# Two-block score stages, plain loads of x, paired tangents and a separate last unit in a gated attention and feed-forward kernel

## The chip, the cores and the metric

The kernel runs on one core of one Trainium2 chip. The metric is the time of one execution on the device in microseconds; before the change the median of three runs is 1058.25 us (1052.69, 1058.25 and 1058.3).

The core has a matrix engine (PE), whose weight loads are listed apart (PEld), a vector engine (DVE), a scalar engine for exponentials and tangents (ACT), GpSimd (POOL) and a sync engine (SP). Each runs its own instructions in order. Matrix products land in PSUM, which has eight banks of 128 x 512 f32 values; everything else lives in SBUF. Transfers are issued from the queues of SP and ACT.

## What is computed

Two branches read the same x (2048 rows of 512, bf16) and are mixed row by row with a gate:

```python
x = A_x
g = _sigmoid((x * gate_w).sum(-1, keepdims=True))
a = _A_ref(x, A_wqkv, A_wo)                  # attention: 32 heads of 16
b = _B_ref(x, B_w1, B_w2, B_w3, B_w4)
return g * a + (1 - g) * b
...
# _B_ref
h = _gelu(_layernorm(x, axis=-1) @ w1)
...
# four quarters of h shifted by 1, -1, 2, -2 rows
hs = jnp.concatenate([g0, g1, g2, g3], axis=-1) @ w2
x1 = x + hs
h2 = _gelu(_layernorm(x1, axis=-1) @ w3) @ w4   # inner width 1792
return x1 + h2
```

Branch A is plain softmax attention over all 2048 rows, followed by the product with `wo`.

## The kernel before

Attention is cut into 32 units: 4 chunks of 512 query rows times 8 groups of 4 heads. A unit runs over 16 tiles of 128 key rows, and for each of them over its 4 heads, so it has 64 blocks. A block is one score product of 128 keys by 512 queries, filling one PSUM bank. All 2048 blocks are laid in one row and cut into slots of three (`SB = 3`): 683 slots. A slot's scores (`scores`, L446) fill a stage of three banks; one ACT instruction (L510) takes the exponential of all three into a bf16 tile `pt`. Two stages exist, so scores of slot i+2 can be made once the exponential of slot i is done. `attend` (L466) multiplies four finished blocks with the values into the accumulator `acc`; a column of ones beside the values yields the softmax denominators.

PSUM is thereby full: two stages of three banks, one bank for `acc` (`psA`), one bank (`psG`, tag `gen`) for all other products: the projections of queries, keys and values, the transposes and products of branch B, and the final product with `wo`.

The order on each engine is the order in which the program's text issues instructions. One loop runs over the slots. In each it issues the exponential, the scores of slot i+2, the attends whose blocks are ready, the postponed work that has come due (`run_due`, list `later`), and then `beside`: it takes steps from generators of other work until a credit is used up. The credit is 1.0 a slot for the first 22 slots and 0.47 after. A generator yields the price of the step that it has just issued: 0.45 for two matmuls of 512 columns (`MM2`), so 0.9 for a projection of four; 1.2 in place of the last 0.45 where a tanh follows. `need` runs whatever is missing at once. `early` issues the value and key projections of the first head group, then the other keys, then branch B (`mlp`). Query projections (`urgent`) come at set slots, and a chunk's final products (`out_tile`) when all its units and its part of branch B are there.

Lines that matter here:

- L91 to L95: weights are loaded from ACT's queue; x arrives transposed (`xT`, four chunks) by transposing transfers on SP's queue. L108: x is also loaded plainly, tile by tile (`x_sb`).
- L129 is the product in `proj` (keys, queries and both first products of branch B), L160 the value product; L137, L150 and L165 empty the bank into `kT`, `qT` (two masked copies) and `vp`.
- L175 to L183 (`ln_stats`): mean and variance of 16 row tiles, one after another, then the root. L195 normalizes, L203 transposes on PE, L204 copies out.
- L212 to L225 (`gelu_evac`): gelu of one 128 x 512 block by a tanh on ACT (L221), with four DVE instructions before it and one after.
- L476 to L492 (`finish_unit`): the accumulator is copied to `accsb`; three transfers bring the denominators into a tile 16 wide, their reciprocals out to memory, and these back, spread over 128 partitions as `bcs`; then the unit's result is scaled into `oT`.
- L324 to L333 (`out_tile`): eight products with `wo` for a row tile, the gate mix on DVE (L329, L331), the store.

After the last slot the kernel finishes the last unit and computes the four `out_tile`s of the last chunk.

Of the kernel before, what the change touches and what calls it, by code (L numbers as in the profile page):

```python
# [15 lines left out]
EPS = 1e-5  # L16
# [5 lines left out]
def kernel(  # L22
# [33 lines left out]
    psS = ctx.enter_context(tc.tile_pool(name="psS", bufs=2, space=bass.MemoryType.PSUM))  # L56
    psA = ctx.enter_context(tc.tile_pool(name="psA", bufs=1, space=bass.MemoryType.PSUM))
    psG = ctx.enter_context(tc.tile_pool(name="psG", bufs=1, space=bass.MemoryType.PSUM))
    dpool = ctx.enter_context(tc.tile_pool(name="dram", bufs=1, space=bass.MemoryType.DRAM))
# [4 lines left out]
    opool = ctx.enter_context(tc.tile_pool(name="opool", bufs=25))  # L64
# [3 lines left out]
    gelp = ctx.enter_context(tc.tile_pool(name="gel", bufs=4))  # L68
    stat = ctx.enter_context(tc.tile_pool(name="stat", bufs=2))
    fin = ctx.enter_context(tc.tile_pool(name="fin", bufs=2))  # L70

# [12 lines left out]
    mask = const.tile([P, 2], F32, name="mask")  # L84
    rec_d = dpool.tile([NC_ * NU, 4, CH], F32, name="rec_d")
# [5 lines left out]
    nc.scalar.dma_start(out=wkv[:, :, 0:D], in_=wview(A_wqkv[:, D:2 * D]))  # L91
    nc.scalar.dma_start(out=wq[:], in_=wview(A_wqkv[:, 0:D]))
    nc.scalar.dma_start(out=wkv[:, :, D:2 * D], in_=wview(A_wqkv[:, 2 * D:3 * D]))
    for c in range(NC_):
        nc.sync.dma_start(out=xT[c][:], in_=x_flat[c * CH:(c + 1) * CH, :], transpose=True)  # L95

    make_identity(nc, ident[:])
# [9 lines left out]
    for t in range(NT):  # L107
        nc.sync.dma_start(out=x_sb[t][:], in_=x_flat[t * P:(t + 1) * P, :])  # L108
# [14 lines left out]
    state = {"slot": 0}  # L123
    later = []
    made = set()

# [7 lines left out]
    def k_proj(G, c):  # L134
        ps = psG.tile([P, CH], F32, tag="gen", name="ps_k")
        yield from proj(ps, wkv, slice(G * P, (G + 1) * P), xT[c])
        nc.vector.tensor_copy(out=kT[G][:, c, :], in_=ps[:])  # L137
        made.add(("k", G, c))
        yield MM2
        yield FREE  # L140
# [3 lines left out]
    def q_proj(c, G):  # L144
        ps = psG.tile([P, CH], F32, tag="gen", name="ps_q")
# [10 lines left out]
    def v_proj(t):  # L156
        ps = psG.tile([P, CH], F32, tag="gen", name="ps_v")
# [13 lines left out]
    def ln_stats(tag, res):  # L171
        mv = const.tile([P, NT, 2], F32, name=f"mv{tag}")
        for t in range(NT):
            st = stat.tile([P, 6], F32, tag="bnst", name="st")
            nc.vector.bn_stats(out=st[:], in_=x_sb[t][:])  # L175
            nc.vector.bn_aggr(out=mv[:, t, :], in_=st[:])
            yield 0.4
            yield FREE
        rstd = const.tile([P, NT], F32, name=f"rstd{tag}")
        mhalf = const.tile([P, NT], F32, name=f"mhalf{tag}")  # L180
        nc.gpsimd.memset(mhalf[:], -0.5)
        nc.vector.tensor_scalar(out=rstd[:], in0=mv[:, :, 1], scalar1=EPS, scalar2=None, op0=ALU.add)
        nc.gpsimd.tensor_tensor(out=rstd[:], in0=rstd[:], in1=mhalf[:], op=ALU.pow)  # L183
        for _ in range(4):
            yield 0.6
            yield FREE
        res += [mv, rstd]

    def norm_T(mv, rstd, c, res):
        xnT = xtpool.tile([P, KT, CH], BF16, tag="xnT", name="xnT")  # L190
        xns = []
        for j in range(4):
            t = 4 * c + j
            xn = xnpool.tile([P, D], BF16, tag="xn", name="xn")
            nc.vector.tensor_scalar(out=xn[:], in0=x_sb[t][:], scalar1=mv[:, t, 0:1],  # L195
                                    scalar2=rstd[:, t:t + 1], op0=ALU.subtract, op1=ALU.mult)
            xns.append(xn)
            yield 0.2
            yield FREE
        for kt in range(KT):  # L200
            pt = psG.tile([P, CH], BF16, tag="gen", name="ps_t")
            for j in range(4):
                nc.tensor.transpose(pt[:, j * P:(j + 1) * P], xns[j][:, kt * P:(kt + 1) * P], ident[:])  # L203
            nc.vector.tensor_copy(out=xnT[:, kt, :], in_=pt[:])  # L204
            yield 0.5
            yield FREE
        res.append(xnT)

    def gelu_evac(ps, dst):
        slot = state["slot"]  # L210
        yh = gelp.tile([P, CH], BF16, tag="yh", name="yh")
        nc.vector.tensor_scalar(out=yh[:], in0=ps[:], scalar1=0.5, scalar2=None, op0=ALU.mult)  # L212
        sq = gelp.tile([P, CH], BF16, tag="sq", name="sq")
        nc.vector.tensor_tensor(out=sq[:], in0=yh[:], in1=yh[:], op=ALU.mult)  # L214
        nc.vector.tensor_scalar(out=sq[:], in0=sq[:], scalar1=8.0 * C2, scalar2=2.0 * C1,
                                op0=ALU.mult, op1=ALU.add)
        nc.vector.tensor_tensor(out=sq[:], in0=sq[:], in1=yh[:], op=ALU.mult)  # L217
        th = gelp.tile([P, CH], BF16, tag="th", name="th")

        def tanh():  # L220
            nc.scalar.activation(out=th[:], in_=sq[:], func=ACT.Tanh)  # L221
            later.append((state["slot"] + 2, gate_up))

        def gate_up():
            nc.vector.scalar_tensor_tensor(out=dst, in0=th[:], scalar=1.0, in1=yh[:],  # L225
                                           op0=ALU.add, op1=ALU.mult)

        later.append((slot + 4, tanh))
# [5 lines left out]
    def gate():  # L234
        for t in range(NT):
            scr = gelp.tile([P, CH], BF16, tag="yh", name="scr")
            nc.vector.tensor_tensor_reduce(
                out=scr[:], in0=x_sb[t][:], in1=gw_b[:], scale=1.0, scalar=0.0,
                op0=ALU.mult, op1=ALU.add, accum_out=g_raw[:, t:t + 1])
            yield 0.4  # L240
            yield FREE
        for _ in range(3):
            yield 0.6
            yield FREE
        nc.scalar.activation(out=g_t[:], in_=g_raw[:], func=ACT.Tanh, scale=0.5)
        for _ in range(3):
            yield 0.6
            yield FREE
        nc.vector.tensor_scalar(out=g_fin[:], in0=g_t[:], scalar1=0.5, scalar2=0.5,
                                op0=ALU.mult, op1=ALU.add)  # L250

    def mlp():
# [3 lines left out]
        yield from gate()  # L256
        res = []
        yield from ln_stats(1, res)
        mv1, rstd1 = res
# [3 lines left out]
        for c in range(NC_):  # L263
            res = []
            yield from norm_T(mv1, rstd1, c, res)
            for m in range(KT):
                ps = psG.tile([P, CH], F32, tag="gen", name="ps_1")
                yield from proj(ps, w12, slice(m * P, (m + 1) * P), res[0])
                gelu_evac(ps, hT[:, m, 2 + c * CH:2 + (c + 1) * CH])
                yield 1.2  # L270
                yield FREE
        for _ in range(5):
            yield 0.6
            yield FREE
        shift = [1, -1, 2, -2]
        for t in range(NT):
            ps = psG.tile([P, CH], F32, tag="gen", name="ps_2")
            for j in range(KT):
                c0 = 2 + t * P - shift[j]
                nc.tensor.matmul(ps[:], lhsT=hT[:, j, c0:c0 + P], rhs=w12[:, j, D:2 * D],  # L280
                                 start=(j == 0), stop=(j == KT - 1))
                if j == 1:
                    yield MM2
            nc.vector.tensor_tensor(out=x_sb[t][:], in0=x_sb[t][:], in1=ps[:], op=ALU.add)
            yield MM2
            yield FREE
        res = []
        yield from ln_stats(2, res)
        mv2, rstd2 = res
        for c in range(NC_):  # L290
            res = []
            yield from norm_T(mv2, rstd2, c, res)
            g2T = hgpool.tile([P, FT, CH], BF16, tag="hg", name="g2T")
            for m in range(FT):
                ps = psG.tile([P, CH], F32, tag="gen", name="ps_3")
                yield from proj(ps, w3, slice(m * P, (m + 1) * P), res[0])
                gelu_evac(ps, g2T[:, m, :])
                yield 1.2
                yield FREE
            for _ in range(5):  # L300
                yield 0.6
                yield FREE
            for j in range(4):
                t = 4 * c + j
                ps = psG.tile([P, CH], F32, tag="gen", name="ps_4")
                for m in range(FT):
                    nc.tensor.matmul(ps[:], lhsT=g2T[:, m, j * P:(j + 1) * P], rhs=w4[:, m, :],  # L307
                                     start=(m == 0), stop=(m == FT - 1))
                    if m % 2 and m < FT - 1:
                        yield MM2  # L310
                nc.vector.tensor_tensor(out=x_sb[t][:], in0=x_sb[t][:], in1=ps[:], op=ALU.add)  # L311
                yield MM2
                yield FREE
# [3 lines left out]
    oTs = {}  # L317
    state["mixable"] = 0

    def out_tile(c, j):  # L320
        t = 4 * c + j
        aps = psG.tile([P, CH], F32, tag="gen", name="ps_o")
# [238 lines left out]
```

## Time and profile before

| | us |
|---|---|
| median of three runs | 1058.25 |
| profiled execution, its own time | 1064.77 |
| its span, first to last instruction | 1063.0 |
| first exponential starts | 17.40 |
| last exponential ends | 1037.84 |
| exponentials, 683 | 939.4 busy, 1.568 each on average |
| tanh, 72 of 128 x 512 | 51.9 busy, 0.721 each on average |

A row of the timeline gives start, duration, engine, line, operation, tiles (out<-in) and shapes, then in brackets the idle time ahead of it and who ended it. Neighbours of one kind are merged (x4), and one instruction can begin while the one ahead of it is still in its last part, so a start-to-start distance says more than a duration. In the row of 40 slices each digit is the busy share of one slice (26.6 us) in tenths.

### The profile page before, as it was taken

Reading aid. Unit: us, or ns where it says so; the run is one execution under the profiler, and the core shown is the slowest. Engines: PE = TensorE matmul, PEld = TensorE weight load, DVE = VectorE, ACT = ScalarE, POOL = GpSimd, SP = SyncE. Lnnn points to the kernel's source line nnn. Section 1 sums busy time; section 2 is a strip of 40 time slices with the busy share of each in tenths; the row PEclk is TensorE's granted clock in tenths of the full one; section 3 lists DMA queues with packets and bytes.
Section 4 is the critical chain, followed back from the end, with each engine's and each line's share of the span. In section 5 each row is a group of like instructions: output and inputs, shape, how many; then the busy total and the mean of one; then the engine's idle time right before and its main releaser. Section 6 shows DMA issues by size and latency. Waiting matters only on the chain.

```text
span 1063.0 us, 12795 instructions
## 1 busy us (share of the span) xinstructions
PE 833.5 (78%) x5120; PEld 227.4 (21%) x5120; DVE 371.7 (35%) x749; ACT 963.2 (91%) x757; POOL 13.3 (1%) x30
## 2 busy tenths in 40 slices
PE   4878778877888788779877788877788887787774
PEld 1122212222222121112222112221122222122111
DVE  1123443444423534531244421345421345411002
ACT  2356999999999999999999999999999999999990
POOL 2000001000000100000000000000000000000000
PEclk9997656677679666879998779988779978879556
DMA  9500100000000000000000000000000000000000
GB/s 230 150 0 11 51 11 1 11 11 11 11 9 5 11 11 11 11 11 11 25 8 11 11 11 11 27 16 1 10 11 11 31 11 11 1 11 12 11 10 31
DMA packets 31803, 22.97 MB, mean 22 GB/s; under 512 B 18048, under 2 KB 27136, under 8 KB 31744
## 3 DMA queue, kind: packets, MB, share of 16 engines
q1 hardware_dynamic: 30160, 20.58, 6.7%
q10 hardware_dynamic: 1584, 1.57, 0.6%
q8 instruction: 40, 0.66, 0.3%
q14 instruction: 19, 0.16, 0.1%
HBM read 17.43 MB, written 2.36 MB: 19 GB/s over the span
## 4 chain that ended last, share of the span: by engine, by line
ACT 48%; issue 25%; PE 21%; DVE 4%; DMA 2%; ACTq 0%; DVEq 0%; SPq 0%
ACT pt L510 44%; PE stage L446 6%; PE acc L466 4%; ACT th L221 4%; PE ps_v L160 2%; PE ps L129 2%; PE ps_k L129 2%; PE ps_q L129 2%; PE ps L307 1%; PE ps_t L203 1%; PE ps_o L324 1%; DMA xT<-in_A_x_dram 1%; DVE vp L165 1%; DVE qT L150 1%; DVE kT L137 1%
## 5 line engine op out<-in xcount | busy, mean ns | idle before, releaser
L510 ACT ACTIVATE pt<-stage 128x1536 bf16<-128x1536 f32 (+1 forms) x683 | 939.4, 1568 | 72.3 <-PE stage L446 70.7
L446 PE MATMUL stage<-qT,kT 32*128 32x512 bf16 x2048 | 326.7, 467 | 173.5 <-ACT pt L510 160.3
L466 PE MATMUL acc<-pt,vp 128*17 128x512 bf16 (+1 forms) x2048 | 244.1, 470 | 0.9 <-ACT pt L510 0.5
L446 PEld LDWEIGHTS <-kT 32*128 32x128 bf16 x2048 | 104.3, 94 | 471.8 <-issue 460.0
L129 PE MATMUL ps<-xnT,w 128*128 128x512 bf16 x288 | 111.0, 476 | 3.7 <-DVE qT L150 3.7
L212 DVE TENSOR_SCALAR yh<-ps 128x512 bf16<-128x512 f32 x72 | 49.8, 692 | 154.2 <-PE ps L129 154.2
L466 PEld LDWEIGHTS <-vp 128*17 128x17 bf16 (+1 forms) x2048 | 50.0, 89 | 157.4 <-issue 157.3
L307 PE MATMUL ps<-w,g2T 128*128 128x512 bf16 x224 | 71.9, 409 | 1.5 <-DVE qT L150 1.1
L476 DVE COPY accsb<-acc 128x512 f32<-128x512 f32 x32 | 22.1, 689 | 94.5 <-PE acc L466 94.5
L221 ACT ACTIVATE th<-sq 128x512 bf16<-128x512 bf16 x72 | 51.9, 721 | 0.0
L324 PE MATMUL ps_o<-wo_pad,oT 128*128 128x512 bf16 x128 | 40.6, 419 | 12.6 <-DVE oT L492 6.9
L311 DVE TENSOR_TENSOR x_sb<-x_sb,ps 128x512 bf16<-128x512 bf16 x16 | 11.0, 688 | 104.4 <-PE ps L307 104.4
L492 DVE TENSOR_TENSOR oT<-accsb,bcs 128x512 bf16<-128x512 f32 x32 | 22.0, 688 | 62.8 <-DMA bcs<-rec_d 62.8
L129 PE MATMUL ps_k<-xT,wkv 128*128 128x512 bf16 x64 | 24.8, 497 | 17.5 <-DMA xT<-in_A_x_dram 11.4
L225 DVE SCALAR_TENSOR_TENSOR g2T<-th,yh 128x512 bf16<-128x512 bf16 x56 | 37.9, 676 | 0.4 <-ACT th L221 0.4
L150 DVE TENSOR_SCALAR qT<-ps_q,mask 128x512 bf16<-128x512 f32 x32 | 22.6, 747 | 38.2 <-PE ps_q L129 38.2
L160 PE MATMUL ps_v<-wkv,xT 128*128 128x512 bf16 x64 | 26.5, 529 | 8.8 <-DVE vp L165 7.8
L217 DVE TENSOR_TENSOR sq<-sq,yh 128x512 bf16<-128x512 bf16 x72 | 30.6, 425 | 2.5
L214 DVE TENSOR_TENSOR sq<-yh 128x512 bf16<-128x512 bf16 x72 | 30.6, 425 | 2.5
L204 DVE COPY xnT<-ps_t 128x512 bf16<-128x512 bf16 x32 | 13.6, 425 | 45.9 <-PE ps_t L203 45.8
L129 PEld LDWEIGHTS <-w 128*128 128x128 bf16 x288 | 17.8, 102 | 49.3 <-issue 49.3
L129 PE MATMUL ps_q<-xT,wq 128*128 128x512 bf16 x64 | 25.5, 496 | 1.9 <-DVE kT L137 1.0
(41 smaller groups left out, 255.7 us busy)
## 6 DMA issues: line engine op xcount, KB each, us to landing
bcs<-rec_d SPq DMA_DIRECT2D x32, 256.0 KB
w<-in_B_w_dram SPq DMA_DIRECT2D x2, 1792.0 KB
x_sb<-in_A_x_dram SPq DMA_DIRECT2D x16, 128.0 KB
out_dram<-ot SPq DMA_DIRECT2D x16, 128.0 KB
wkv<-in_A_wqkv_dram ACTq DMA_DIRECT2D x2, 512.0 KB
w<-in_B_w_dram SPq DMA_DIRECT2D x2, 512.0 KB
wq<-in_A_wqkv_dram ACTq DMA_DIRECT2D x1, 512.0 KB
wo_pad<-in_A_wo_dram SPq DMA_DIRECT2D x8, 64.0 KB
```

Of the source, the lines that this page charges most:

```text
L129: nc.tensor.matmul(ps[:], lhsT=wt[:, kt, wsl], rhs=rhs[:, kt, :], start=(kt == 0), stop=(kt == KT - 1))
L150: nc.vector.tensor_scalar(out=qT[:, a, :], in0=ps[:], scalar1=mask[:, a:a + 1], scalar2=None, op0=ALU.mult)
L160: nc.tensor.matmul(ps[:], lhsT=xT[c][:, kt, o:o + P], rhs=wkv[:, kt, D:2 * D], start=(kt == 0), stop=(kt == KT - 1))
L212: nc.vector.tensor_scalar(out=yh[:], in0=ps[:], scalar1=0.5, scalar2=None, op0=ALU.mult)
L214: nc.vector.tensor_tensor(out=sq[:], in0=yh[:], in1=yh[:], op=ALU.mult)
L221: nc.scalar.activation(out=th[:], in_=sq[:], func=ACT.Tanh)
L225: nc.vector.scalar_tensor_tensor(out=dst, in0=th[:], scalar=1.0, in1=yh[:], op0=ALU.add, op1=ALU.mult)
L307: nc.tensor.matmul(ps[:], lhsT=g2T[:, m, j * P:(j + 1) * P], rhs=w4[:, m, :], start=(m == 0), stop=(m == FT - 1))
L324: nc.tensor.matmul(aps[:], lhsT=oTs[(c, u)][:, j * P:(j + 1) * P], rhs=wo_pad[:, u, :], start=(u == 0), stop=(u == NU - 1))
L446: nc.tensor.matmul(st[:, k * CH:(k + 1) * CH], lhsT=kT[G][32 * j:32 * j + 32, cc, o:o + P], rhs=qTs[(c, G)][32 * j:32 * j + 32, a, :], sta ...
L466: nc.tensor.matmul(acc[32 * j:32 * j + M, :], lhsT=lhsT, rhs=pts[i][:, k * CH:(k + 1) * CH], start=(kt == 0), stop=(kt == NT - 1), skip_gr ...
L510: nc.scalar.activation(out=pt[:, 0:w], in_=stages.pop(i)[:, 0:w], func=ACT.Exp, scale=DH ** -0.5)
```

## The change

Eight banks are divided anew at first, and several other parts are rearranged:

- For the first 34 slots (`EARLY`) a slot has two blocks, so the two stages need four banks. The two banks set free (`psX`) serve, with `psG`, the projections: `gen` gives out the three in turn. At slot 34 the pools are closed and the old stages of three banks are opened. There are 694 slots in all.
- Four row tiles of x are loaded first, two on each queue, then the 128 columns of the query and key weights that the first head group needs. The first chunk of `xT` is made by 16 transposes on PE, copied out by ACT and DVE in turn; the other three chunks come by transposing transfers as before. The rest of the weights follows in two more transfers. Fourteen matmuls on a tile of zeros (`idle`) run ahead of the transposes.
- Branch B's gelu works on two blocks at once (`gelu_pair`): DVE and ACT instructions of 1024 columns, issued one, two, five and seven slots later; the tanh writes over its input.
- Statistics, gate sums and normalizations are put on a list (`asides`) of which one entry is issued per slot from slot 34 on; the root is taken per four row tiles. `wait_for` yields empty steps until something is made.
- The credit per slot is 0.6 for the first 34 slots, then 0.36, and 1.0 once branch B is done. A tanh is no longer priced.
- The last chunk's final products sum seven units beside the last unit's slots (into `parts`, f32); the last unit (`finish_all`) has its denominators spread by one f32 matmul with a matrix of ones and zeros (`spread`), reciprocals and products by halves on DVE, and one product per row tile (`last_tile`), each in a PSUM buffer of its own, stored from two queues.

```diff
-    for c in range(NC_):
+    for t in range(4):
+        (nc.sync, nc.scalar)[t % 2].dma_start(out=x_sb[t][:], in_=x_flat[t * P:(t + 1) * P, :])
+    nc.sync.dma_start(out=wq[:, :, 0:P], in_=wview(A_wqkv[:, 0:P]))
+    nc.scalar.dma_start(out=wkv[:, :, 0:P], in_=wview(A_wqkv[:, D:D + P]))
     nc.scalar.dma_start(out=wkv[:, :, D:2 * D], in_=wview(A_wqkv[:, 2 * D:3 * D]))
+    for c in range(1, NC_):
         nc.sync.dma_start(out=xT[c][:], in_=x_flat[c * CH:(c + 1) * CH, :], transpose=True)
+    nc.scalar.dma_start(out=wkv[:, :, P:D], in_=wview(A_wqkv[:, D + P:2 * D]))
+    nc.scalar.dma_start(out=wq[:, :, P:D], in_=wview(A_wqkv[:, P:D]))
...
+    EARLY = 34
+    def gen(name, dtype=F32):
+        state["gen"] += 1
+        if state["young"] and state["gen"] % 3:
+            return psX.tile([P, CH], dtype, tag="x", name=name)
+        return psG.tile([P, CH], dtype, tag="gen", name=name)
...
+    def gelu_pair(w, m, rhs, dst, key):
+        yh = gelp.tile([P, 2, CH], BF16, tag="yh", name="yh")
+        sq = gelp.tile([P, 2, CH], BF16, tag="sq", name="sq")
+        for r in range(2):
+            ps = gen("ps_y")
+            yield from proj(ps, w, slice((m + r) * P, (m + r + 1) * P), rhs)
+            nc.vector.tensor_scalar(out=yh[:, r, :], in0=ps[:], scalar1=0.5, scalar2=None, op0=ALU.mult)
+            if r == 0:
+                yield MM2
+                yield FREE
...
+        def tanh():
+            nc.scalar.activation(out=sq[:], in_=sq[:], func=ACT.Tanh)
+        def gate_up():
+            nc.vector.scalar_tensor_tensor(out=dst, in0=sq[:], scalar=1.0, in1=yh[:], op0=ALU.add, op1=ALU.mult)
+            made.add(key)
+        slot = state["slot"]
+        later.extend([(slot + 1, square), (slot + 2, inner), (slot + 5, tanh), (slot + 7, gate_up)])
+        yield MM2
+        yield FREE
...
+    def last_tile(j, aps):
+        c, u = NC_ - 1, NU - 1
+        t = 4 * c + j
+        nc.tensor.matmul(aps, lhsT=oTs[(c, u)][:, j * P:(j + 1) * P], rhs=wo_pad[:, u, :],
+                         start=True, stop=True)
+        ot = otp.tile([P, CH], BF16, tag="ot", name="ot")
+        nc.vector.scalar_tensor_tensor(out=ot[:], in0=aps, scalar=g_fin[:, t:t + 1], in1=parts[0][:, j, :],
+                                       op0=ALU.mult, op1=ALU.add)
+        (nc.sync, nc.scalar)[j % 2].dma_start(out=out_flat[t * P:(t + 1) * P, :], in_=ot[:])
...
+        if asides and s >= EARLY:
+            asides.popleft()()
...
+    while i < len(row):
+        w = 2 if len(slots) < EARLY else 3
+        slots.append((i, row[i:i + w]))
+        i += w
...
+        if k == EARLY:
+            expo(k - 1)
+            to_free()
+            young.close()
+            state["young"] = False
+            old["psS"] = ctx.enter_context(tc.tile_pool(name="psS", bufs=2, space=bass.MemoryType.PSUM))
...
+    def finish_all(accsb, oT):
+        to_free()
+        while later or outs:
+            state["slot"] += 1
+            run_due()
+            if outs and not later:
+                drive(out_tile(*outs.popleft()))
+        bc = psG.tile([P, CH], F32, tag="gen", name="bc")
+        nc.tensor.matmul(bc[:], lhsT=spread[:], rhs=accsb[:], start=True, stop=True)
+        rr = npool.tile([P, CH], F32, tag="bcs", name="rr")
+        for n in range(2):
+            half = slice(n * CH // 2, (n + 1) * CH // 2)
+            nc.vector.reciprocal(out=rr[:, half], in_=bc[:, half])
+            nc.vector.tensor_tensor(out=oT[:, half], in0=accsb[:, half], in1=rr[:, half], op=ALU.mult)
...
+    warm = psA.tile([P, CH], F32, tag="acc", name="warm")
+    for _ in range(14):
+        nc.tensor.matmul(warm[:], lhsT=idle[:, 0:P], rhs=idle[:, 0:CH], start=True, stop=True)
+    for kt in range(KT):
+        pt = gen("ps_t", BF16)
+        for j in range(4):
+            nc.tensor.transpose(pt[:, j * P:(j + 1) * P], x_sb[j][:, kt * P:(kt + 1) * P], ident[:])
+        if kt % 2:
+            nc.scalar.activation(out=xT[0][:, kt, :], in_=pt[:], func=ACT.Copy)
+        else:
+            nc.vector.tensor_copy(out=xT[0][:, kt, :], in_=pt[:])
+    drive(q_proj(0, 0))
     drive(k_proj(0, 0))
-    drive(q_proj(0, 0))
     scores(0)
     scores(1)
...
-        credit = beside(min(credit, 0.0) + (1.0 if i < 22 else 0.47))
+        credit = beside(min(credit, 0.0) + (0.6 if i < EARLY else 1.0 if state["done"] else 0.36))
```

## The prediction

> **What bounds the kernel now.** I read the page's first two parts, then a table of two stages, then ScalarE's waits, then the timeline at both ends. ScalarE (ACT) is the busy engine, and the slices say where it is not:
>
> ```profile
> PE 833.5 (78%) x5120; PEld 227.4 (21%) x5120; DVE 371.7 (35%) x749; ACT 963.2 (91%) x757; POOL 13.3 (1%) x30
> ACT  2356999999999999999999999999999999999990
> ```
>
> ACT is short of work only in the first four slices and the last. Cut where that ends, the stage table (length, then busy time of PE, PEld, DVE, ACT, POOL, then clock) reads:
>
> ```profile
> 17.00:95.60 78.60, 62.45 (x252) 14.51 (x245) 18.96 (x28) 36.04 (x25) 0.00 (x0) 0.91 0.29 82
> 95.60:1037.80 942.20, 755.63 (x4830) 207.88 (x4827) 343.25 (x706) 925.86 (x731) 5.95 (x5) 0.79 0.04 13
> ```
>
> The waits of ACT in those two stages (us in total, times, longest) name one releaser:
>
> ```profile
> ACT pt L510 <- PE stage L446: 55.8, 23, 13.8
> ACT pt L510 <- PE stage L446: 14.9, 31, 1.5
> ```
>
> So the span of 1063.0 is: 17.4 until the first exponential, 961.9 of ACT work (36.04 + 925.86), 58.5 in which ACT waits for scores (42.2 before 95.6, 16.3 after), and 25.2 behind the last exponential, which ends at 1037.84. Only the second term is ScalarE's own.
>
> The timeline shows why the first stage starves:
>
> ```profile
> 39.57 1.01 PE L160 MATMUL ps_v<-wkv,xT 128*128 128x512 bf16 x2 [0.78 <-DVE vp L165]
> 40.51 0.61 PE L446 MATMUL stage<-qT,kT 32*128 32x512 bf16 x3
> 41.05 0.61 PE L466 MATMUL acc<-pt,vp 128*17 128x512 bf16 x4
> 58.22 1.87 PE L160 MATMUL ps_v<-wkv,xT 128*128 128x512 bf16 x4 [0.78 <-DVE vp L165]
> 60.02 0.61 PE L446 MATMUL stage<-qT,kT 32*128 32x512 bf16 x3
> 65.58 1.02 PE L160 MATMUL ps_v<-wkv,xT 128*128 128x512 bf16 x4 [0.46 <-DVE vp L165]
> 66.53 0.39 PE L446 MATMUL stage<-qT,kT 32*128 32x512 bf16 x3
> 66.86 0.39 PE L466 MATMUL acc<-pt,vp 128*17 128x512 bf16 x4
> ```
>
> Two things are to be seen. Every projection waits 0.78 us until VectorE (DVE) has emptied the single spare bank, and scores queue behind it. And the same four matmuls take 1.80 us from start to next start at 58.22, but 0.95 at 65.58: PE runs at half speed until about 62 us (the stage table's 0.91 doesn't show that; the rows do). From rows like these I use: slow PE clock, scores 0.54, four attends 0.54, a projection 1.80; fast clock, 0.33, 0.32 and 0.95.
>
> The end, after the last exponential:
>
> ```profile
> 1037.90 0.60 PE L466 MATMUL acc<-pt,vp 128*17 128x512 bf16 x2 [0.31 <-ACT pt L510]
> 1038.53 0.69 DVE L476 COPY accsb<-acc 128x512 f32<-128x512 f32 x1 [17.55 <-PE acc L466]
> 1039.25 0.53 SPq L478 DMA_DIRECT2D den<-accsb  x1
> 1042.90 0.54 SPq L488 DMA_DIRECT2D bcs<-rec_d  x1
> 1047.77 0.69 DVE L492 TENSOR_TENSOR oT<-accsb,bcs 128x512 bf16<-128x512 f32 x1 [6.35 <-DMA bcs<-rec_d]
> 1059.40 0.75 DVE L331 SCALAR_TENSOR_TENSOR ot<-dd,g_fin,x_sb 128x512 bf16<-128x512 f32 x1
> ```
>
> 8.5 us pass in three transfers for the denominators (1039.25 to 1047.77), 12 in four output tiles one after another through one bank, 2.85 in the last store.
>
> **The start.** x comes by plain loads and is transposed on PE, in place of a transposing transfer that lands at 11.39. Fourteen dummy matmuls from about 1.0 at 0.43 end at 7.0. The x tiles should be there: the first 512 KB weight of the old order released its waiter at 4.96. Four groups of four transposes (0.54 a group, the slow rows of L203) alternate between DVE copies (0.43) and ACT copies (about 0.61, priced by the 0.64 tanh): last copy at 9.8. The last query matmul ends near 10.2, two mask products (0.75 each) 11.7, the key copy (0.69) 12.5, scores 0.66 as before: first exponential near 13.0, 4.4 earlier. Bounds: 12 if the dummies already run fast, 17.4 if x lands as late as the old transposing transfer. On ACT's queue two more weight issues (0.53 each) stand before the table load (1.28), and wait for x tiles; with x at 5 they are through by 7.4, before the first ACT copy at 8.1. On SP's queue the transfer for the second x chunk is now behind three issues (about 2.0 instead of 0.7). With the old 10.7 it lands near 12.7; its key projection comes near 16. The cover is 3 us; beyond it PE, and all scores behind, wait.
>
> **The first 34 slots.** Each is two blocks, at 0.6 credit, so 0.67 projections (0.9 credit each). A fast slot costs PE 0.33 + half of 0.32 + 0.67 x 0.95 = 1.13; a slow one 0.54 + 0.27 + 1.20 = 2.01. ACT needs 0.93 for 1024 columns: a 1536 exponential advances 1.348 back to back (25 from 1004.04 to 1037.84, the last 1.45 long, so 24 steps in 32.35), a 512 tanh 0.52 (row below), hence 0.81 ns a column, and 1.348 - 512 x 0.81 ns. PE is the bound either way. With three banks PE no longer stops for each copy, stays full, and should reach the fast clock as it did near 62, after the first stretch without a gap (from 58.22). 34 x 1.13 = 38.4, plus 3 for places where an attend directly follows its own value copy, plus 3 for the first slow slots: 44.4, against 31.7 of ACT work. Idle 12.7 in place of the old 42.2. Swapping the bank pools at slot 34 drains two buffers: 1.5 more, between 0 and 3.
>
> [...] No row here shows transposes after dummies.
>
> **ACT's own work.** The tanh rows:
>
> ```profile
> 183.51 0.64 ACT L221 ACTIVATE th<-sq 128x512 bf16<-128x512 bf16 x1
> 184.03 4.15 ACT L510 ACTIVATE pt<-stage 128x1536 bf16<-128x1536 f32 x3
> ```
>
> A tanh advances 0.52; of 1024 columns 0.93. After: 34 x 0.93 + 660 x 1.348 + 36 x 0.93 + 0.3 = 955.1, against 961.9. Eleven more exponentials cost less than 36 fewer tanhs give.
>
> **The middle.** Rate 0.36 a slot, 0.40 projections. Slow PE: 0.54 + 0.75 x 0.54 + 0.40 x 1.80 = 1.67 a slot against 1.35 to 1.53 on ACT; fast: 0.95. PE falls behind a little, fills up, turns fast, recovers. Before, a feed-forward projection cost 1.65 credits of 0.47 (0.28 a slot), those of the second feed-forward product 0.9 (0.52): bursts, and ACT's 16 idle us sit in them. More even feeding should give about 9; the last chunk's seven-unit sums, now at rate 1.0 beside the last unit's slots, cost 3. I take 12, between 4 and 25. Statistics and the gate, one per slot, add at most 0.85 to DVE in a slot of 1.35: free while DVE has a third of its time busy; without that cover, 0.85 a slot is late in emptying the one bank.
>
> **The end.** From the last exponential: attends 0.7, copy 0.69, an f32 matmul, two reciprocals and two products by halves, four final products of 0.75, a store 2.85. No row has an f32 matmul: between one slow bf16 matmul (0.43) and eight (3.4); I take four, both operands being twice as wide, 1.7 and 0.2 to pass on. The wide reciprocal has one near row:
>
> ```profile
> L486 DVE RECIPROCAL rec<-den 128x16 f32<-128x16 f32 x32 | 7.9, 248 | 15.1 <-DMA den<-accsb 14.9
> L182 DVE TENSOR_SCALAR rstd<-mv 128x16 f32<-128x16 f32 x2 | 0.3, 170 | 0.0
> ```
>
> 78 ns more on 16 columns are 4.9 ns a column above the plain 1: for 256 columns 1.7 at most and 0.42 at least (half of 0.69); I take 1.7, since the row shows the surplus. Two halves with products: 2 x (1.7 + 0.42) = 4.3. Sum 0.7 + 0.7 + 1.9 + 4.3 + 3.0 + 2.9 = 13.5, bounds 9.5 and 16, against 25.2.
> [...]
>
> **Sum.** 13.0 + 955.1 + (12.7 + 1.5 + 12) + 13.5 = 1007.8, 55.2 under 1063.0. The profiled run is 0.6% above the median; I subtract from the median: 1058.25 - 55.2 = 1003.
>
> **Rivals.**
> - Slow early clock. PE stays slow for the 34 slots: 34 x 2.01 + 3 = 71.3, 27 more: 1030. For it: in the old stage PE was busy 62 of 79 us and slow for most. Against: its stops were the 0.78 waits that three banks remove.
> - ACT never starves: early idle 6, middle 4, quick reciprocal: 17 less, 986. For it: the old 95.6 to 112 has almost no wait at a higher rate. Against: 1.13 is above 0.93.
> - Slower: DVE late for the one bank. After slot 34 some 175 groups (projections, transposes, sums) still share one bank, and DVE gets instructions of 1024 columns (the gate product 0.68 becomes about 1.2) ahead of the copies. If each group cost the early 0.78, that is 136 us: 1139. It decides from 55 / 175 = 0.32 us a group. For it: DVE runs in order, and scores queue behind the projection. Against: after 100 us PE now waits only some 13 us for DVE in all, because a slot of scores lies between two groups; the halves are still a slot apart.
>
> **Chances.** Forecast 0.63 (own range 992 to 1016), slow clock 0.15, never starved 0.13, late DVE 0.09. The range 985 to 1030 leaves out most of the last and the ends of others. Faster 0.91, and of the late-DVE case 0.02 ends within 0.5%, 0.07 slower. 0.5% is about what a measurement here can tell.
>
> **What would show it.** First exponential near 13; 34 exponentials of 1024 within about 45 us; projections of four in 0.95 there, not 1.80; ACT's waits for scores after that near 12; tanh of 1024 near 1.05; the wide reciprocal near 1.7; tail near 13.5. Wrong if projection rows stay at 1.80, if the second key projection waits for its transfer, or if PE's waits for DVE grow beyond 50 us.

## The result, and the profile after

The changed kernel took 1011.98 us in the median of four runs (1006.66 to 1014.85), the kernel before 1055.47 beside it: ratio 0.9584, 95% interval 0.9529 to 0.9639, so 38 to 50 us less. Repeated later in five runs it took 1013.02 against 1052.69 (0.9618, 0.9585 to 0.965). The forecast of 1003 lies 9 to 10 us below, inside its range of 985 to 1030. The profiled execution is the fastest of the first four: span 1004.9, own time 1006.66.

The first two parts of its page, engine totals and slices:

```profile
PE 784.0 (78%) x5152; PEld 230.4 (23%) x5152; DVE 357.5 (36%) x620; ACT 960.0 (96%) x734; POOL 16.2 (2%) x40
...
ACT  4889999999999999999999999999999999999984
...
PEclk9997687799899799989999998999989975555566
```

ACT is short of work only in the first slice, a little in the next two, and in the last two. The last row is the granted clock of PE in tenths of full speed (9 stands for 90% or more). It is of use further down: its slow tail begins at slice 33 (804 us), where branch B ends (its last product with the second weight of the feed-forward starts at 813).

The stage table, cut at the first exponential, at the first one of 1536 columns and at the end of the last (length, then busy time of PE, PEld, DVE, ACT, POOL, then granted clock, 1.00 being full speed):

```profile
11.21:56.23 45.02, 40.42 (x220) 10.91 (x220) 15.82 (x23) 33.45 (x35) 0.00 (x0) 0.96 0.64 171
56.23:991.57 935.34, 730.71 (x4882) 215.13 (x4881) 330.56 (x580) 924.08 (x697) 8.19 (x10) 0.85 0.04 13
991.57:1004.90 13.33, 4.75 (x9) 0.85 (x8) 7.61 (x9) 0.00 (x0) 0.00 (x0) 0.50 0.11 39
```

Length less ACT's busy time is ACT's idle time: 11.6 in the first stage, 11.3 in the second. With the 11.2 ahead of them, 957.5 of ACT work and 13.3 behind, that is the span.

PE's timeline in the first stage (start, duration, idle time ahead in brackets), and ScalarE's waits:

```profile
39.97 0.39 PE L543 MATMUL acc<-pt,vp 128*17 128x512 bf16 x4
40.30 0.61 PE L182 MATMUL ps_v<-wkv,xT 128*128 128x512 bf16 x2
40.83 0.39 PE L515 MATMUL stage<-qT,kT 32*128 32x512 bf16 x2
...
42.34 1.04 PE L182 MATMUL ps_v<-wkv,xT 128*128 128x512 bf16 x4
43.31 0.39 PE L515 MATMUL stage<-qT,kT 32*128 32x512 bf16 x2
```

```profile
ACT pt L526 <- PE stage L515: 24.2, 36, 3.5
```

No bracket is left: the 0.78 us in which each projection waited for the bank are gone, and four matmuls take 0.97 from start to next start (42.34 to 43.31). ScalarE's waits for scores went from 70.7 to 24.2 us, the wait ahead of the first exponential (13.8 and 3.5) included in both.

The end, VectorE's timeline:

```profile
992.27 0.69 DVE L553 COPY accsb<-acc 128x512 f32<-128x512 f32 x1 [6.70 <-PE acc L543]
995.12 1.76 DVE L590 RECIPROCAL rr<-bc 128x256 f32<-128x256 f32 x1 [2.17 <-PE bc L586]
996.92 0.42 DVE L591 TENSOR_TENSOR oT<-accsb,rr 128x256 bf16<-128x256 f32 x1
997.26 1.75 DVE L590 RECIPROCAL rr<-bc 128x256 f32<-128x256 f32 x1
999.04 0.43 DVE L591 TENSOR_TENSOR oT<-accsb,rr 128x256 bf16<-128x256 f32 x1
999.39 2.72 DVE L395 SCALAR_TENSOR_TENSOR ot<-aps,g_fin,parts 128x512 bf16<-128x512 f32 x4
```

The two reciprocals are 3.5 of the 13.3 us; the f32 matmul lies in the 2.17 ahead of the first. No transfer is left but the store.

### The profile page after: what moved, and what is told of

Its sections match the earlier page's. It is cut to its first block, busy times and chain, and to the rows that moved or that the text cites. A ratio compares the mean times of both kernels' runs of the same rounds, so it can differ in the third digit from the quotient of the medians.

```text
span 1004.9 us, 12720 instructions
## 1 busy us (share of the span) xinstructions
PE 784.0 (78%) x5152; PEld 230.4 (23%) x5152; DVE 357.5 (36%) x620; ACT 960.0 (96%) x734; POOL 16.2 (2%) x40
## 4 chain that ended last, share of the span: by engine, by line
ACT 58%; issue 27%; PE 12%; DVE 2%; DMA 1%; SPq 0%; DVEq 0%; ACTq 0%
ACT pt L526 55%; PE stage L515 4%; ACT sq L259 3%; PE acc L543 2%; PE ps_v L182 2%; PE ps L312 1%; PE ps_y L151 1%; PE ps_o L368 1%; PE ps_k L151 1%; PE ps_q L151 1%; DMA wq<-in_A_wqkv_dram 1%; DVE rr L590 0%; DVE vp L187 0%; DVE dd L373 0%; PE bc L586 0%
## 5 line engine op out<-in xcount | busy, mean ns | idle before, releaser
L526 ACT ACTIVATE pt<-stage 128x1536 bf16<-128x1536 f32 (+1 forms) x694 | 933.0, 1584 | 26.3 <-PE stage L515 24.2
L515 PE MATMUL stage<-qT,kT 32*128 32x512 bf16 x2048 | 313.8, 441 | 190.1 <-ACT pt L526 170.5
L543 PE MATMUL acc<-pt,vp 128*17 128x512 bf16 (+1 forms) x2048 | 231.1, 445 | 3.4 <-DVE vp L187 2.4
L151 PE MATMUL ps_y<-xnT,w 128*128 128x512 bf16 x288 | 95.9, 418 | 7.1 <-DVE yh L245 3.2
L245 DVE TENSOR_SCALAR yh<-ps_y 128x512 bf16<-128x512 f32 x72 | 49.7, 691 | 110.6 <-PE ps_y L151 110.6
L259 ACT ACTIVATE sq<-sq 128x1024 bf16<-128x1024 bf16 x36 | 43.3, 1203 | 0.0
L262 DVE SCALAR_TENSOR_TENSOR g2T<-sq,yh 128x1024 bf16<-128x1024 bf16 x28 | 34.1, 1218 | 0.9 <-ACT sq L259 0.9
L373 DVE TENSOR_TENSOR dd<-ps_o,x_sb 128x512 f32<-128x512 f32 x16 | 11.1, 691 | 56.8 <-PE ps_o L368 56.8
L233 DVE COPY xnT<-ps_t 128x512 bf16<-128x512 bf16 x32 | 13.5, 423 | 34.3 <-PE ps_t L232 34.3
L256 DVE TENSOR_TENSOR sq<-sq,yh 128x1024 bf16<-128x1024 bf16 x36 | 24.9, 692 | 1.2
L251 DVE TENSOR_TENSOR sq<-yh 128x1024 bf16<-128x1024 bf16 x36 | 24.7, 687 | 1.0
L201 DVE BATCH_NORM_STATS2 st<-x_sb 128x6 f32<-128x512 bf16 x32 | 21.8, 682 | 0.4
```

Of the source, the lines that this page charges most:

```text
L151: nc.tensor.matmul(ps[:], lhsT=wt[:, kt, wsl], rhs=rhs[:, kt, :], start=(kt == 0), stop=(kt == KT - 1))
L245: nc.vector.tensor_scalar(out=yh[:, r, :], in0=ps[:], scalar1=0.5, scalar2=None, op0=ALU.mult)
L259: nc.scalar.activation(out=sq[:], in_=sq[:], func=ACT.Tanh)
L262: nc.vector.scalar_tensor_tensor(out=dst, in0=sq[:], scalar=1.0, in1=yh[:], op0=ALU.add, op1=ALU.mult)
L515: nc.tensor.matmul(st[:, n * CH:(n + 1) * CH], lhsT=kT[G][32 * j:32 * j + 32, cc, o:o + P], rhs=qTs[(c, G)][32 * j:32 * j + 32, a, :], sta ...
L526: nc.scalar.activation(out=pt[:, 0:w], in_=stages.pop(k)[:, 0:w], func=ACT.Exp, scale=DH ** -0.5)
```

## The experiments

Unless said otherwise each is the changed kernel with one edit, and a difference is one of medians to its 1011.98 in the first measurement.

**The spare banks alone taken away.** All projections go through the one bank again, in narrow slots.

```diff
-        if state["young"] and state["gen"] % 3:
+        if False:
```

> The changed kernel with all early projections in the one bank psG; the two spare banks stay unused. Theory (three banks keep PE from stopping for each copy): the early stage from first exponential to the end of the 34th, 44.0 us in the changed kernel, grows by 22.7 projections x 0.78 us = 17.7 to about 62, and more (up to 86) if the gaps let the PE clock fall; the time rises by 18 us or more. Rival (it is the dummies and the fast clock that shorten the stage, not the banks): the stage stays under 50 and the time rises by at most 5.

1053.05 (ten runs, 1050.47 to 1058.07), ratio to before 0.9975 (0.9938 to 1.0011): 41 us given back. Its early stage in the stage table, and PE there:

```profile
14.21:94.30 80.09, 68.81 (x216) 12.62 (x215) 15.07 (x22) 34.57 (x34) 0.00 (x0) 0.50 0.30 86
```

```profile
40.77 1.01 PE L182 MATMUL ps_v<-wkv,xT 128*128 128x512 bf16 x2 [0.78 <-DVE kT L159]
41.71 0.61 PE L515 MATMUL stage<-qT,kT 32*128 32x512 bf16 x2
42.25 1.03 PE L182 MATMUL ps_v<-wkv,xT 128*128 128x512 bf16 x2
43.22 0.61 PE L515 MATMUL stage<-qT,kT 32*128 32x512 bf16 x2
```

Up to the end of the 34th exponential this stage takes 80.1 us, where the changed kernel took 44.0 for as many instructions. The 0.78 is back, and two matmuls take 0.94 to 0.97 from start to start. The waits and the slow clock come back together, so what each of them costs is not separated here. The first exponential comes at 14.21 instead of 11.21: 3 of the 41 us are lost ahead of the slots, where the first products wait for the one bank too.

**Wide slots from the start, one bank, credit 1.0 at first.** The division of the banks before, in an otherwise changed kernel. `EARLY` becomes 23, as many slots as these blocks then fill, so the list of asides starts there; no pools are swapped.

```diff
-        w = 2 if len(slots) < EARLY else 3
+        w = 3
...
-        credit = beside(min(credit, 0.0) + (0.6 if i < EARLY else 1.0 if state["done"] else 0.36))
+        credit = beside(min(credit, 0.0) + (1.0 if i < 22 else 1.0 if state["done"] else 0.36))
```

> The changed kernel with stages of three blocks from the start, one bank for projections and the old credit of 1.0 for 22 slots; loads, dummies, pairs, credit later and tail as changed. Theory (narrow stages and spare banks are the largest part, 28 to 30 us): the first 23 slots (69 blocks) take 70 to 80 us in place of 44, the time rises by 26 to 34. Rival (the warm start alone would have shortened this stage): 23 slots in about 57 us, the time rises by about 14.

1033.98 (0.9774, 0.9702 to 0.9846), 22 more, between the 26 to 34 and the 14 of the two expectations. Its first 23 slots took 65.9 us, and its first exponential came at 14.27, as with one bank above. So narrow slots with one bank are worse than wide ones with one bank (by 19 us); it is the two banks set free that pay.

**One dummy matmul in place of fourteen.**

```diff
-    for _ in range(14):
+    for _ in range(1):
```

> The changed kernel with one dummy matmul in place of fourteen. Theory (the dummies bring the fast clock to the first projections): the first query and key products take 1.86 each in place of 1.04, the first exponential comes near 13 in place of 11.2, the first slots are slow for one or two windows, together 4 to 8 us more. Rival (the clock falls behind the transposes anyway, as it did at 14.6 in the changed kernel, and recovers by itself when PE is full): first exponential within 1 us of 11.2, time the same within 2.

1011.62 (1010.00 to 1014.39): no difference, where 4 to 8 more were expected. First exponential at 11.68, early stage to 59.05. No run shows a length for the "windows" that the expectation counts; the clock was at 0.50 from 14 to 22 us here, and from 14 to 24 in the changed kernel's repetition with all fourteen. The dummies are worth nothing that stands out from the spread of the runs.

**The loads in the old order,** x by transposing transfers alone, no transposes on PE.

```diff
-    for t in range(4):
-        (nc.sync, nc.scalar)[t % 2].dma_start(out=x_sb[t][:], in_=x_flat[t * P:(t + 1) * P, :])
...
-    for c in range(1, NC_):
+    for c in range(NC_):
         nc.sync.dma_start(out=xT[c][:], in_=x_flat[c * CH:(c + 1) * CH, :], transpose=True)
```

> The changed kernel with the old loads: whole weights first on ACT's queue, all four chunks of transposed x by transposing transfers, x itself after; no transposes on PE at the start. Theory (the start is worth its whole advance, since nothing later can make it up): first exponential near 17 in place of 11.2 to 11.7, time 5 to 6 us more. Rival (later stages absorb it, or the first products wait for other weights anyway): time within 2 us.

1017.69 (0.9664, 0.9625 to 0.9703), 5.7 more; first exponential at 15.81 instead of 11.21, which is 4.6 of it. The two intervals overlap a little, but the fastest of these four runs, 1016.66, is slower than all nine of the changed kernel (1006.37 to 1014.85).

**The old ending:** the last unit like the others, the last chunk's sums of eight units after it.

```diff
-        if (c, u) == units[-1]:
-            finish_all(accsb, oT)
-            return
...
+    while outs or later or not current["free"] or not state["done"]:
+        state["slot"] += 1
+        run_due()
+        beside(1.0 if later or not state["done"] else 100.0)
```

> The changed kernel with the old end: the last unit's denominators by three transfers, and the last chunk's row tiles summed over eight units behind the last slot. Theory: the stretch behind the last exponential is 25 in place of 13.3, and 4 us of ACT waits in the last 36 us go away with the seven-unit sums: 7 to 8 more in all. Rival (the sums beside the last unit were free): 12 more.

1023.99 (0.9683, 0.9617 to 0.9749), 12 more. The trace shows 27.1 us behind the last exponential instead of 13.3, less 4.4 in which ScalarE no longer waits beside the seven-unit sums: 9.4. So the mechanism of the theory is there, though the total is the 12 of the rival; in this execution the first 34 slots were also slower (49.8 against 45.0; the clock was at 0.50 from 14 to 28 us, in the changed kernel at 0.66 from 14 to 16 and 0.50 from 16 to 18). In VectorE's timeline the first three output tiles follow one another by some 4.4 us, the last by 2.7:

```profile
1006.89 0.69 DVE L373 TENSOR_TENSOR dd<-ps_o,x_sb 128x512 f32<-128x512 f32 x1 [0.70 <-PE ps_o L368]
...
1011.25 0.69 DVE L373 TENSOR_TENSOR dd<-ps_o,x_sb 128x512 f32<-128x512 f32 x1 [2.88 <-PE ps_o L368]
```

**Other credits after slot 34,** 0.47 and 0.32 for 0.36.

```diff
-1.0 if state["done"] else 0.36
+1.0 if state["done"] else 0.47
```

> The changed kernel with 0.47 credit per slot in place of 0.36 after slot 34. Theory (denser bursts of other work make ACT wait for scores): ACT's waits after the early stage grow from about 12 to 16 to 20 us, time 4 to 8 more. Rival (PE has the same work in all, so the rate does not matter): waits within 3 us of 12, time within 2.

1028.91 (0.977, 0.9731 to 0.9809), 17 more where 4 to 8 were expected. ScalarE's waits for scores after the early stage were 23.1 us, where 16 to 20 were expected.

> The changed kernel with 0.32 credit per slot. Theory of the bursts: waits a little lower, 8 to 11, branch B ends later but before the last unit, time 0 to 3 less. Rival (rate does not matter): the same within 2.

1020.85 (0.9704, 0.9656 to 0.9751), 9 more where 0 to 3 less were expected, with 20.7 us of waits in place of 8 to 11. The first expectation had the direction right and the size wrong, the second not even the direction: more other work per slot loses, and less loses too. With 0.47 branch B's last product starts at 657, and the stage table there reads:

```profile
550.00:650.00 100.00, 81.40 (x549) 24.43 (x548) 43.50 (x65) 99.70 (x78) 0.00 (x0) 0.95 0.04 14
650.00:750.00 100.00, 77.21 (x459) 19.52 (x457) 9.17 (x16) 98.03 (x73) 0.00 (x0) 0.56 0.03 9
```

PE is busy for nearly the same share in both lines, and its clock falls from 0.95 to 0.56 when branch B's products are gone. So it is doubtful that the clock follows how busy PE is.

**More narrow work on PE:** the first score product of every slot made twice after slot 34, 659 matmuls more, with the same result.

```diff
+            for _ in range(2 if n == 0 and k > EARLY else 1):
                 nc.tensor.matmul(st[:, n * CH:(n + 1) * CH],
```

> The changed kernel with the first score product of every slot after the 35th made twice, into the same bank with the same values: useless work of 0.2 to 0.43 us a slot on PE. Theory (ACT's waits in the middle and the spread between executions come from stretches at the slow PE clock, and a fuller PE keeps the fast clock): mean clock above 0.95 in place of 0.835 to 0.85, waits after the early stage under 6 in place of 12, time 4 to 8 less, executions within 3 us of each other. Rival (PE's amount of work sets the waits): waits grow, time 5 or more up.

The four runs took 1114.70, 1132.03, 1147.34 and 1154.96 (median 1139.68); even the fastest is 103 above the changed kernel. The profile is of the slowest. Its mean clock was 0.72, where the theory had above 0.95: that a fuller PE keeps the fast clock fell.

**As many matmuls in the same places, but through the full array:** 128 rows instead of 32, thrown away as before.

```diff
+            if n == 0 and k > EARLY:
+                nc.tensor.matmul(st[:, n * CH:(n + 1) * CH],
+                                 lhsT=kT[G][:, cc, o:o + P],
+                                 rhs=qTs[(c, G)][:, a, :],
+                                 start=True, stop=True)
```

> As many extra matmuls in the same places as in the run with each first score made twice (659, 128x512, thrown away), but these use all 128 rows of the array instead of 32. Theory (the granted clock follows how much of the array works, not how long TensorE is busy): the clock after the early stage rises from 0.85 to 0.93 or more, a group of one extra matmul and three scores costs about 0.55 us against the 0.96 of the narrow run in its slow stretches, ScalarE waits for scores no more than 15 us after the early stage, time within 10 us of the changed kernel's 1012. Rival (the amount of TensorE work alone sets it: 659 more matmuls at 0.22 to 0.4 us are 145 to 260 us that do not fit): the clock stays at 0.85 or less and the time is 60 us or more above the changed kernel, as with narrow ones (1115 to 1155).

1023.41 (1019.51 to 1027.44), ratio to before 0.9724 (0.9686 to 0.9763): 91 us less than the fastest run with the narrow ones and 116 less than their median, 10 to 11 more than the changed kernel. One window of the stage table, 360 to 500, for the narrow ones, with a window ahead of it:

```profile
250.00:350.00 100.00, 87.40 (x629) 22.18 (x622) 55.13 (x104) 99.56 (x76) 4.40 (x4) 1.00 0.04 12
360.00:500.00 140.00, 140.00 (x591) 21.85 (x590) 21.99 (x37) 99.07 (x70) 0.00 (x0) 0.50 0.03 9
```

the full ones:

```profile
360.00:500.00 140.00, 126.18 (x853) 35.64 (x851) 51.86 (x82) 139.15 (x106) 0.00 (x0) 0.99 0.05 15
```

and the changed kernel:

```profile
360.00:500.00 140.00, 109.07 (x760) 33.41 (x759) 52.53 (x83) 139.71 (x107) 0.00 (x0) 0.95 0.05 15
```

From 360 to 500, with narrow extra work, PE never stops for 140 us, its clock stays at 0.50, and ACT starves (99 of 140 us busy). This is not narrow work alone: 99 of the 591 matmuls are full products of branch B, the query projections and the output tiles. Nor does this mix always run slowly: from 250 to 350, with 106 full products among 629, the same execution ran at 1.00. It goes back and forth between long fast and long slow stretches. With full extra work PE gets 0.99, does 853 matmuls in place of 591 (248 of them full), and still has 14 us to spare; in steps of 100 us its clock is 0.98 to 1.00 from 150 to 750. The timelines show the two clocks in single instructions, the narrow ones first (four scores, the first of them twice), then the full ones:

```profile
399.47 1.06 PE L516 MATMUL stage<-qT,kT 32*128 32x512 bf16 x4
400.46 0.61 PE L544 MATMUL acc<-pt,vp 128*17 128x512 bf16 x4
```

```profile
400.71 0.38 PE L516 MATMUL stage<-qT,kT 128*128 128x512 bf16 x1
401.02 0.39 PE L520 MATMUL stage<-qT,kT 32*128 32x512 bf16 x3
401.35 0.39 PE L548 MATMUL acc<-pt,vp 128*17 128x512 bf16 x4
```

0.99 from start to start against 0.64 (400.71 to 401.35) for as many matmuls. The mean clock was 0.92 instead of 0.85. In size the expectation missed narrowly throughout: clock 0.92 for 0.93, a group 0.64 for 0.55, 11 us above 1012 for 10, and ScalarE's waits after the early stage 18.5 against the 15 allowed, 12.0 of them after 760, where branch B ends (its last product starts at 813.5) and the clock was 0.86 from 750 to 850, then 0.68 and 0.65 even so. So, while branch B ran, the clock stayed up with extra products through the full array (0.99 from 360 to 500) where it did not with as many narrow ones in the same places (0.50); but here their own cost is more than the few us of waits that they could save. Full products are not all that counts: in the early stage with one bank 88 of 216 matmuls were full ones and filled some 44.9 of the 80.1 us (an estimate: 22 projections at the 1.01 and 1.03 of its rows), and the clock was 0.50.

**The changed kernel repeated,** five runs.

> The changed kernel once more, unchanged, for its spread. Theory (identical instructions, but the clock's phases fall otherwise from run to run): its runs spread over 5 to 10 us, the shorter spans at the higher mean clock (0.85 with 1005, 0.835 with 1013 earlier), and in this profile the early stage is not 44.0 us again but anything between 43 and 50. Rival (the spread comes from elsewhere, such as transfers or the chip): spans do not follow the clock.

Spans 1004.6, 1010.8, 1011.2, 1012.8 and 1012.8 at mean clocks of 0.847, 0.839, 0.836, 0.836 and 0.833: the order of the spans is that of the clocks. Its profile, cut as the first was:

```profile
11.92:59.29 47.37, 43.01 (x220) 11.12 (x220) 15.82 (x23) 33.62 (x34) 0.00 (x0) 0.89 0.58 158
59.29:997.53 938.24, 736.52 (x4882) 216.04 (x4881) 330.42 (x580) 924.43 (x697) 8.18 (x10) 0.84 0.04 13
```

The same instructions, but an early stage of 47.4 instead of 45.0 at a clock of 0.89 instead of 0.96. In seven profiles with these same early instructions it was 43.7, 43.7, 45.0, 47.4, 49.7, 49.8 and 49.8: the two at 43.7 ran at full clock throughout, and the one with credit 0.47, for instance, reads:

```profile
11.13:60.88 49.75, 45.52 (x220) 11.35 (x220) 15.82 (x23) 33.62 (x34) 0.00 (x0) 0.83 0.58 155
```

**Two small edits on top:** the first key projection ahead of the first query projection, and 0.6 instead of 1.0 while the last chunk's sums are made.

```diff
-    drive(q_proj(0, 0))
     drive(k_proj(0, 0))
+    drive(q_proj(0, 0))
...
-        credit = beside(min(credit, 0.0) + (0.6 if i < EARLY else 1.0 if state["done"] else 0.36))
+        credit = beside(min(credit, 0.0) + (0.6 if i < EARLY or outs and outs[0][0] == NC_ - 1 else 1.0 if state["done"] else 0.36))
```

> The changed kernel with two small edits: the first k projection ahead of the first q projection, so that the copy of k and the second masked copy of q leave the path to the first exponential; and a credit of 0.6 instead of 1.0 while the last chunk's seven-unit sums are made. Theory: first exponential at about 10 us (11.2 before the edit), ScalarE's waits in the last 36 us at most 2 us (4.4 before), together 2 to 4 us less: 1008 to 1010 beside a changed kernel at 1012. Rival (both are inside the spread that the clock makes from run to run, 8 us): no difference from the changed kernel that its repetition in this call does not show as well.

1007.87 (1006.60 to 1010.75), ratio to before 0.958 (0.9553 to 0.9607), beside the repetition's 1013.02: 5 us less, while the intervals of the two ratios overlap (0.9585 to 0.965 for the repetition). What can be seen is the end. ScalarE in the changed kernel, where the sums are made:

```profile
973.67 1.45 ACT L526 ACTIVATE pt<-stage 128x1536 bf16<-128x1536 f32 x1 [1.84 <-PE stage L515]
976.13 2.79 ACT L526 ACTIVATE pt<-stage 128x1536 bf16<-128x1536 f32 x2 [1.00 <-PE stage L515]
979.77 1.45 ACT L526 ACTIVATE pt<-stage 128x1536 bf16<-128x1536 f32 x1 [0.84 <-PE stage L515]
981.60 1.45 ACT L526 ACTIVATE pt<-stage 128x1536 bf16<-128x1536 f32 x1 [0.38 <-PE stage L515]
983.40 8.16 ACT L526 ACTIVATE pt<-stage 128x1536 bf16<-128x1536 f32 x6 [0.35 <-PE stage L515]
```

and with the edits:

```profile
978.73 1.45 ACT L526 ACTIVATE pt<-stage 128x1536 bf16<-128x1536 f32 x1 [0.98 <-PE stage L515]
980.40 13.54 ACT L526 ACTIVATE pt<-stage 128x1536 bf16<-128x1536 f32 x10 [0.22 <-PE stage L515]
```

The brackets sum to 4.4 and 1.2: 3.2 us saved. The first exponential came at 11.49, not at 10 as hoped: that lies between the changed kernel's two profiles (11.21 and 11.92). It is the fastest version measured here, by its median; how much faster than the changed kernel is not settled by ten runs.

## Why the prediction was right, and where its numbers missed

Direction and mechanism held, except for the reason given for the middle. By the prediction's own terms, in us:

| | before | predicted | changed | repeated |
|---|---|---|---|---|
| to the first exponential | 17.4 | 13.0 | 11.2 | 11.9 |
| ACT's work | 961.9 | 955.1 | 957.5 | 958.0 |
| early idle, with the swap | 42.2 | 14.2 | 11.6 | 13.7 |
| later idle | 16.3 | 12 | 11.3 | 13.8 |
| behind the last exponential | 25.2 | 13.5 | 13.3 | 13.3 |
| span | 1063.0 | 1007.8 | 1004.9 | 1010.8 |

- **The sum against its base** is the step that failed: "The profiled run is 0.6% above the median; I subtract from the median: 1058.25 - 55.2 = 1003." The terms after the change were worked out one by one; their sum, 1007.8 and the 1.8 that lie around the span, is 1009.6, 2.4 and 3.4 under the two medians and inside the spread of the nine runs (1006.37 to 1014.85). Subtracting from the median took 6.5 us (1064.77 less 1058.25) off once more, and 1003 lies below all nine. That the terms owed little to what made the profiled execution slow is argued, not tested.
- **The first 34 slots.** Right in size and cause: 45.9 with the swap against 45.0 and 47.4, projections at 0.97, the swap 1.1. The spare banks carry it: without them 41 us of the gain are gone. Three parts undone singly cost 22 (banks and slots), 12 (ending) and 5.7 (loads), together 40 of the 43.5. The paired tangents and the list of asides were not undone singly.
- **The start** was 1 to 2 us better than forecast. The old loads lose 4.6 of it, close to the 4.4 that the forecast gave to the loads and transposes; but 3 us more hang on the spare banks, which the forecast did not price there. No row before had transposes after dummies; here the 16 took 1.28 us in all, not 0.54 a group, and the first projection behind them ran at the fast clock (1.00 from 6 to 10 us; 0.87 from start to start, 7.64 to 8.51). The dummies add nothing to the start that can be measured.
- **ACT's work** came out 2.4 to 2.9 above. Most of it is the 34 exponentials of 1024: they kept ACT busy for 33.45 us, 0.98 each, where the forecast had 0.93 each, 31.6. The 0.93 is the step of a row without gaps; an exponential that ACT has waited for counts with its whole length, 1.02. The tanh of 1024 is as forecast where it can be read: the shortest takes 1.05, and at 182.53 and 201.62 the next exponential starts 0.94 and 0.95 later. The mean duration of 1203 ns is no measure of that step: before, the tanh of 512 that the forecast stepped by 0.52 had a mean of 721.

```profile
L259 ACT ACTIVATE sq<-sq 128x1024 bf16<-128x1024 bf16 x36 | 43.3, 1203 | 0.0
```

- **The end** is right in sum and in parts: reciprocals 1.75 each (1.7 by the row of 16 columns), f32 matmul with its handing on 2.2 (1.9, with four slow bf16 matmuls as the author's estimate between one and eight; the trace has 2.07 for it).
- **"PE falls behind a little, fills up, turns fast, recovers"** was the reason given for the middle, and it does not hold, so that the 12 us came out by luck. Filling up alone did not turn PE fast: with narrow extra work it was full for 140 us and stayed at 0.50. In the changed kernel it does recover while branch B runs (0.57 from 100 to 120 us, 0.94 from 120 to 140), but from 820 to 960 it stays at 0.50 to 0.59, three quarters busy. That the clock was higher beside full products explains in part why, of the three rates measured, the middle one was best. From 110 to 410 the clock was 0.82 with 0.32, 0.87 to 0.89 in five profiles with 0.36, and 0.92 with 0.47. But 0.36 spreads branch B's full products until 813 us, and 0.47 leaves the last 370 without them. Of the 27 us that ScalarE waited for PE with 0.47 after the early stage, 12.7 fall into this last part; 14.4 fall ahead of it, at the high clock, as the theory of the bursts has it. That 0.32 loses by its lower clock is argued only.
- **The rivals.** The slow early clock (1030) is what happened with one bank (0.50 in its early stage), which then took 1053; in part it happened in five of the seven profiles with three, at 0.50 for some 3 us (the changed kernel's, 14.6 to 18) to 17. Never starved (986) did not come: even at full clock the early stage was 43.7. The late DVE did not come: no line's waits of PE for VectorE sum to more than 3.4 us in the trace, and that line is in the tail.

Open: what exactly the clock follows, since nearly the same mix ran at 1.00 and at 0.50 in one execution; whether it is the rows (32 of 128 for scores) or the columns (17 of 128 for attends) that keep it low; and whether matmuls in PE's two holes ahead of the first slots (1.24 us before 10.78, 1.11 before 12.28) would hold the early stage at 43.7. No run here shows any of them.

## What to carry to other kernels

When a sum is made term by term for the changed kernel, trust the sum itself; a difference to one profiled execution, taken off a median, counts the distance between the two a second time. Before pricing a stage of small matmuls, read which clock such a stage ran at (here, with credit 0.47, 0.95 beside branch B's full products and 0.56 after them), and try full products spread among them before finishing these early (after them ScalarE waited 12.7 us for PE). More buffers where one engine waits for another to empty the only one were worth more here (22 us for banks and slots) than a wider instruction on the busiest engine (the tangents, about 4 by the prediction's steps of 0.52 and 0.93, an estimate).

## What was not expected of the hardware

- PE was busy without a gap for 140 us at half clock (0.50) when most of its work was score products of 32 rows and attends of 17 columns, with 99 full products among 591 matmuls. With 659 extra matmuls through all 128 rows in place of 659 narrow ones it ran at 0.99 there, and the kernel took at least 91 us less.
- Nearly the same mix ran at 1.00 from 250 to 350 and at 0.50 from 360 to 500 in one execution.
- The length of the same first 34 slots depends on the run: 43.7 to 49.8, with the clock of that stage between 1.00 and 0.83.
- A reciprocal of 256 f32 columns takes 1.75 us, 6.9 ns a column, against 0.42 for a product of the same shape.
